# A state-space layer with a ReGLU network behind it: order and size of the first weight transfers, and the engine of one cast

## The chip, the cores and the metric

The kernel runs on one core of a Trainium2 chip. The core has TensorE (PE, the matrix engine, with its weight loads PEld), VectorE (DVE), ScalarE (ACT), GpSimd (POOL) and SyncE (SP), which run their own instruction streams beside each other, and 16 DMA engines that all queues share. The metric is the device time of one execution in microseconds (us).

## The reference, cut to what matters

Two stages. The first is a chunked state-space layer (batch 4, 8 heads, 768 positions, head size 32, state size 16). The second takes its output as 3072 tokens of 256 features through a gated network with 1536 hidden features.

```python
# first stage, per chunk of positions: cum = cumulative sum of log(a)
L = np.exp(cum[:, :, :, None] - cum[:, :, None, :]) * causal
CB = np.einsum('bhin,bhjn->bhij', Cc, Bc)
y_intra = np.einsum('bhij,bhjd->bhid', CB * L, xc)
y_inter = np.einsum('bhin,bhnd->bhid', Cc, state) * np.exp(cum)[:, :, :, None]
y[:, :, sl] = y_intra + y_inter
state = decay_full[:, :, None, None] * state + np.sum(Bx, axis=2)
...
# second stage
gate = np.maximum(x @ w_gate, 0.0)
val = x @ w_val
return (gate * val @ w_out).astype(np.float32)
```

All inputs and the output are float32; the kernel multiplies in bfloat16.

## The kernel before, in words

**Stages.** The 3072 tokens are 12 *pairs* of 256 (a pair is two chunks of 128) and 6 *blocks* of 512 (two pairs). The first stage turns B, C and x of a pair into `yT`, the transposed bfloat16 input of the second stage. For a pair, B and C are scaled by decay factors (`scale_bc`, tile `bs`), transposed on TensorE (`transp`, line 389) and copied out as `BT` and `CT` (`bevac`, `cevac`); `G` (line 452) makes the products `g` of all position pairs; `gevac` copies them out as `gs` with the causal mask, quarter 0 and half of quarter 1 by ACT (lines 464 and 472) followed by POOL's `affine_select` (line 171, "the selects"), the rest by DVE in one instruction per piece (line 475). `Dm` (line 630) multiplies `gs` with x, `inter` (line 610 or 619) adds what the running state gives, `astep` (line 509) and `sevac` carry the state on, and `yevac` copies the sum into `yT`.

**The second stage** runs, for a block, over 12 *steps* f of 128 hidden features: gate and value matmuls, ReLU on ACT, the product on DVE into `h`; then `fout` (line 783) multiplies `h` with `wo`. `gv` (line 738) does a step for 512 tokens, `gvh_mm` (line 753) for 256. In block 0 the first half of steps 0 to 3 is woven into the first stage of pair 1, the second half follows, and then steps 4 to 11 run for 512 tokens each in the order of f.

**Weights.** They lie in DRAM as float32 and are cast to bfloat16 in the transfer, on POOL's DMA queue. `weights(g)` (line 150) loads group g of gate weights, then group g of value weights; a group is 256 columns, that is steps 2g and 2g+1, in a tile of its own `[128, 2, 256]`. `w_tile(ws, f, k)` picks the 128 columns of step f from its group. `weights_out` (line 160) loads a third of `wo`. A matmul that reads a tile waits until the whole transfer into that tile has landed.

**Order.** `in_order` (line 15) ties every instruction to the one before it on its engine, so the program's text is the order on each engine, POOL's DMA issues among them. SP's queue carries a, B, C and x; ACT issues three of pair 0's and pair 1's loads. On POOL the text gives, for the start: the masks; groups 0 and 1 (line 226, held until the first scan of a is done by the small cast in line 225); the cast of x of pair 0, first half (line 845, with `x_cast`, line 841; the second half is DVE's, line 844); two selects of pair 0; a quarter of `scale_bc` of pair 1 (line 893); `weights(2)` and the gate part of group 3 (lines 894 and 895); two selects of pair 1; the value part of group 3, groups 4 and 5 (lines 922 to 924); the three parts of `wo`; then the scaling of pairs 2 and 3, the zeroing of three tiles, and the cast of x of pair 2. On ACT the text has, around line 845: the copies of `BT` and of half of `CT` of pair 0, then the first `gs` cast of pair 0, the copy `bx`, the second `gs` cast. x of pair 1 is issued by SP in `load_x1` (line 866) and cast by ACT in line 921.

Of the kernel before, what the change touches and what calls it, by code (L numbers as in the profile page):

```python
# [9 lines left out]
BF16 = mybir.dt.bfloat16  # L10
# [19 lines left out]
def kernel(  # L30
# [13 lines left out]
    nc = tc.nc  # L44
# [5 lines left out]
    DM, DF = moe_w_gate.shape  # L50
    T = NB * S
    NF = DF // 128
# [5 lines left out]
    glob = ctx.enter_context(tc.tile_pool(name="glob", bufs=1))  # L58
# [78 lines left out]
    def new_xb(p):  # L137
        xb = att.tile([128, 2 * NH * D], BF16, tag="xb", name="xb", bufs=6)
        st.setdefault(p, {})["x"] = [xb[:, i * NH * D:(i + 1) * NH * D] for i in range(2)]
# [3 lines left out]

    wgs, wvs = ([glob.tile([128, 2, 256], BF16, name="%s%d" % (w, g)) for g in range(NF // 2)]
                for w in ("wg", "wv"))
    wo = glob.tile([128, NF, DM], BF16)

    def weights(g, which=(0, 1)):  # L150
        for k in which:
            w, src = ((wgs, moe_w_gate), (wvs, moe_w_val))[k]
            nc.gpsimd.dma_start(
                out=w[g],
                in_=src[:, g * 256:(g + 1) * 256].rearrange("(k p) f -> p k f", k=2))

    def w_tile(ws, f, k):
        return ws[f // 2][:, k, f % 2:256:2]

    def weights_out(f0, f1):  # L160
        nc.gpsimd.dma_start(
            out=wo[:, f0:f1].rearrange("p (g j) m -> p g (j m)", j=2),
            in_=moe_w_out[f0 * 128:f1 * 128, :].rearrange("(g p j) m -> p g (j m)", p=128, j=2))
# [32 lines left out]
    w = mm.tile([128, 512], FP32, tag="y", name="w")  # L196
# [27 lines left out]

    nc.gpsimd.tensor_copy(out=wgs[0][0:1, 0, 0:1], in_=cp_first[0:1, 0:1])
    weights(0)
    weights(1)

    fac = glob.tile([128, NB, NC, 2, 8], FP32)
# [78 lines left out]
    def new_bs(p):  # L308
        st[p]["bs"] = att.tile([128, 4, 128], BF16, tag="bs", name="bs", bufs=6)
        bs = st[p]["bs"]  # L310
        if p < NWIDE:
            st[p]["tin"] = [[bs[:, 2 * j + r] for r in range(2)] for j in range(2)]
        else:
            st[p]["tin"] = [[bs[:, 2 * i + j] for i in range(2)] for j in range(2)]
            st[p]["B"] = st[p]["tin"][0]

    def copy(eng, out, in_):
        (eng.copy if eng is nc.scalar else eng.tensor_copy)(out=out, in_=in_)  # L318
# [15 lines left out]
    def scale_bc(p, eng, js=slice(0, 2), f=None, ts=(0, 1)):  # L334
        b, c0, _ = place(p)
        src, dst = views(p, js)
        if f is None:
            if p < NWIDE:
                f = wfac[:, p, js].rearrange("s j r h -> s (j r) h")
            else:  # L340
                f = fac[:, b, c0:c0 + 2].rearrange("s c j h -> s (c j) h")
        n = f.shape[1]
        for t in ts:
            eng.tensor_tensor(  # L344
                out=dst[:, :, t], in0=src[:, :, t],
                in1=f[:, :, 4 * t:4 * t + 4].to_broadcast([128, n, 4, N]), op=ALU.mult)
# [384 lines left out]
    def gv(b, f, turns=False):  # L731
        if b not in fst:
            fst[b] = ffn.tile([128, NF, 512], BF16, tag="h", name="h")
        tk = slice(b * 512, (b + 1) * 512)
        g, v = bank("gate"), bank("val")
        order = [(g, wgs, 0), (g, wgs, 1), (v, wvs, 0), (v, wvs, 1)]
        for o, ws, k in sorted(order, key=lambda e: e[2]) if turns else order:
            nc.tensor.matmul(out=o, lhsT=w_tile(ws, f, k), rhs=yT[:, k, tk],  # L738
                             start=(k == 0), stop=(k == 1), skip_group_check=True)
        r = ffn.tile([128, 512], BF16, tag="r", name="r", bufs=4)  # L740
        nc.scalar.activation(r, g, AF.Relu)  # L741
        nc.vector.tensor_tensor(out=fst[b][:, f], in0=r, in1=v, op=ALU.mult)  # L742

    def gvh_mm(b, f, u):
        if f == 0 and u == 0:
            fst[b] = ffn.tile([128, NF, 512], BF16, tag="h", name="h")
        tk = slice(b * 512 + u * 256, b * 512 + (u + 1) * 256)
        gv_ = (mm.tile([128, 2, 256], FP32, tag="y", name="gv") if b + f == 0 else
               bank("gv", (128, 2, 256)))
        jk = [(j, k) for j in range(2) for k in range(2)]  # L750
        early = b + f + u == 0
        for j, k in sorted(jk, key=lambda v: v[1]) if early else jk:
            nc.tensor.matmul(out=gv_[:, j], lhsT=w_tile((wgs, wvs)[j], f, k), rhs=yT[:, k, tk],  # L753
                             start=(k == 0 and not (early and j)), stop=(k == 1),
                             skip_group_check=True)
        fst[b, f, u] = gv_
# [84 lines left out]
    def x_cast(p, i, eng):  # L841
        copy(eng, st[p]["x"][i], st[p]["xr"][:, i].rearrange("s h d -> s (h d)"))

    x_cast(0, 1, nc.vector)
    x_cast(0, 0, nc.gpsimd)
    new_bs(1)
    keep_warm(1)
    keep_warm(1, 256)
# [42 lines left out]
    scale_bc(1, nc.vector, C_)  # L891
    scale_bc(1, nc.vector, B_, ts=(0,))
    scale_bc(1, nc.gpsimd, B_, ts=(1,))
    weights(2)
    weights(3, (0,))
    new_xb(1)
    Dm(0, "shared")
    inter(0, 1)
# [20 lines left out]
    gevac(1, early=True, between=lambda: backevac(1, nc.scalar))  # L919
    for i in range(2):  # L920
        x_cast(1, i, nc.scalar)
    weights(3, (1,))
    weights(4)
    weights(5)
    weights_out(0, 4)
    weights_out(4, 8)
    weights_out(8, NF)
# [26 lines left out]
    for w in range(W3):  # L954
        nc.scalar.copy(
            out=fac[:, :, 2 * w:2 * w + 2, 1, :].rearrange("p b i h -> p i b h"),
            in_=dall[:, :, w])
# [198 lines left out]
```

## Time and profile before

| what | value |
|---|---|
| median of 3 runs | 122.5 us (122.35, 122.5, 123.0) |
| the profiled execution, whole | 122.54 us |
| its span in the trace | 120.8 us |
| DMA moved in the span | 13.69 MB in 80591 packets |
| q1, SP's queue | 10.54 MB, 58.5% of 16 engines' span |
| q0, POOL's queue | 2.36 MB, 14.1% |
| gate and value transfers | 12 of 128 KB (bfloat16), median 5.0 and 5.1 us from issue to landing |
| `wo` transfers | 3 of 256 KB, median 7.1 us |

Times in the trace count from the start of the span. A timeline line gives start, duration, engine, line of the kernel, operation, tiles written and read, and in brackets how long the engine was idle before it and what ended that idle time. `POOLq`, `SPq` and `ACTq` are the DMA issues of the engines; an issue's own duration is the time the engine spends on it, not the time of the transfer. "To landing" is the time from the start of the issue until the last part of the transfer has arrived.

### The profile page before, as it was taken

The numbers are of one execution on the slowest core, as the hardware profiler recorded it, in microseconds if no ns is written. First come the engines' busy times: TensorE is split into PE (matmuls) and PEld (weight loads), VectorE is DVE, ScalarE is ACT, GpSimd is POOL, SyncE is SP. The second block draws the span as 40 slices with busy tenths as digits, with TensorE's granted clock in tenths as the row PEclk, the third lists the DMA queues.
The fourth block names the chain that finished last, engine by engine and source line by source line (L and its number), as shares of the span: only waits on it lengthen the run. The fifth ranks groups of instructions, "written<-read, shape, count | busy, mean of one in ns | idle before, by whom it ended". The sixth has DMA issues, their size and how long they took to land.

```text
span 120.8 us, 3330 instructions
## 1 busy us (share of the span) xinstructions
PE 116.8 (97%) x1238; PEld 75.1 (62%) x1238; DVE 89.2 (74%) x214; ACT 74.3 (61%) x161; POOL 51.4 (43%) x104
## 2 busy tenths in 40 slices
PE   7999999999999999999999999999999999999990
PEld 2446854577885477888487544578444677444790
DVE  5898879986999956899875687856778675678500
ACT  4077886752998734888734767526767445766240
POOL 6879999741805342957076273333400033000000
PEclk9999999999999999999999999999999999999999
DMA  2999999999998999999986799962200002200022
GB/s 57 215 186 176 192 173 197 211 144 127 159 125 151 133 101 109 121 242 134 98 148 121 84 122 149 194 130 82 91 5 0 0 0 92 87 0 0 0 87 87
DMA packets 80591, 13.69 MB, mean 113 GB/s; under 512 B 73424, under 2 KB 80576, under 8 KB 80576
## 3 DMA queue, kind: packets, MB, share of 16 engines
q1 hardware_dynamic: 73088, 10.54, 58.5%
q0 software_dynamic: 4080, 2.36, 14.1%
q10 hardware_dynamic: 3408, 0.59, 2.6%
q8 instruction: 9, 0.15, 0.5%
q14 instruction: 6, 0.05, 0.1%
HBM read 11.12 MB, written 3.15 MB: 118 GB/s over the span
## 4 chain that ended last, share of the span: by engine, by line
PE 94%; DVE 3%; ACT 0%; issue 0%; DVEq 0%
PE o L783 26%; PE gate L738 19%; PE val L738 19%; PE gv L753 13%; PE w L200 3%; PE g L452 2%; PE g L491 2%; PE y L678 1%; PE y L630 1%; PE o L795 1%; PE tp L389 1%; DVE gs L475 1%; DVE bs L344 1%; PE y L619 1%; PE y L665 0%; PE dw L236 0%
## 5 line engine op out<-in xcount | busy, mean ns | idle before, releaser
L742 DVE TENSOR_TENSOR h<-r,val 128x512 bf16<-128x512 bf16 x54 | 36.7, 687 | 9.3 <-ACT r L741 6.4
L741 ACT ACTIVATE r<-gate 128x512 bf16<-128x512 f32 x54 | 32.2, 597 | 11.9 <-PE gate L738 10.9
L783 PE MATMUL o<-wo,h 128*128 128x256 bf16 x276 | 33.6, 273 | 0.0
L738 PE MATMUL val<-yT,wv 128*128 128x512 bf16 x108 | 32.6, 379 | 0.0
L738 PE MATMUL gate<-yT,wg 128*128 128x512 bf16 x108 | 32.6, 379 | 0.0
L783 PEld LDWEIGHTS <-h 128*128 128x128 bf16 x276 | 25.8, 98 | 5.5 <-issue 1.2
L171 POOL TENSOR_SCALAR_AFFINE_SELECT gs<-gs 128x512 bf16<-128x512 bf16 (+1 forms) x24 | 12.2, 533 | 24.9 <-ACT gs L464 24.9
L475 DVE TENSOR_TENSOR gs<-g,masks 128x512 bf16<-128x512 f32 x24 | 15.4, 685 | 5.9 <-PE g L491 2.8
L738 PEld LDWEIGHTS <-wv 128*128 128x128 bf16 x108 | 10.6, 98 | 12.5 <-DMA wv<-in_moe_w_val_dram 0.2
L738 PEld LDWEIGHTS <-wg 128*128 128x128 bf16 x108 | 10.4, 98 | 11.1
L464 ACT CAST gs<-g 128x512 bf16<-128x512 f32 x12 | 7.0, 587 | 14.7 <-PE g L452 6.4
L763 DVE TENSOR_TENSOR h<-r,gv 128x256 bf16<-128x256 bf16 x36 | 13.9, 417 | 0.9 <-ACT r L760 0.7
L760 ACT ACTIVATE r<-gv 128x256 bf16<-128x256 f32 x36 | 13.7, 389 | 1.2
L753 PE MATMUL gv<-yT,wg 128*128 128x256 bf16 x72 | 13.9, 273 | 0.0
L753 PE MATMUL gv<-yT,wv 128*128 128x256 bf16 x72 | 13.9, 272 | 0.0
L297 POOL TENSOR_TENSOR bz<-bcr,fac 128x512 bf16<-128x512 f32 x6 | 6.4, 1059 | 10.5 <-DMA bcr<-in_B_dram 10.5
L811 ACT COPY ob<-o 128x512 f32<-128x512 f32 x11 | 6.5, 592 | 4.1 <-PE o L783 4.0
L318 ACT CAST yT<-y 128x512 bf16<-128x512 f32 (+1 forms) x9 | 4.6, 531 | 5.4 <-PE y L678 3.4
L753 PEld LDWEIGHTS <-wv 128*128 128x128 bf16 x72 | 7.0, 98 | 0.8
L753 PEld LDWEIGHTS <-wg 128*128 128x128 bf16 x72 | 6.8, 98 | 1.1 <-issue 0.2
L200 PE MATMUL w<-const-bfloat16-1.0 128*128 128x512 bf16 (+3 forms) x16 | 6.0, 497 | 0.8 <-PEq L1140 0.8
L318 DVE CAST yT<-y 128x256 bf16<-128x256 f32 (+1 forms) x7 | 3.7, 548 | 4.0 <-PE y L678 2.0
(119 smaller groups left out, 112.0 us busy)
## 6 DMA issues: line engine op xcount, KB each, us to landing
xr<-in_x_dram SPq DMA_DIRECT2D x23, 128.0 KB, 3.2
out_dram<-ob SPq DMA_DIRECT2D x9, 256.0 KB, 2.7
bcr<-in_B_dram SPq DMA_DIRECT2D x16, 64.0 KB, 3.0
bcr<-in_C_dram SPq DMA_DIRECT2D x16, 64.0 KB, 2.9
wg<-in_moe_w_gate_dram POOLq DMA_DIRECT2D x6, 128.0 KB, 5.0
wv<-in_moe_w_val_dram POOLq DMA_DIRECT2D x6, 128.0 KB, 5.1
wo<-in_moe_w_out_dram POOLq DMA_DIRECT2D x3, 256.0 KB, 7.1
out_dram<-ob SPq DMA_DIRECT2D x4, 128.0 KB, 2.3
```

Of the source, the lines that this page charges most:

```text
L171: nc.gpsimd.affine_select(out=dst, in_=dst, pattern=pattern, compare_op=ALU.is_ge, fill=0.0, base=0, channel_multiplier=-1)
L200: nc.tensor.matmul(out=w[:, 0:cols], lhsT=nc.const_aps.tensor(1.0, [128, 128], BF16), rhs=nc.const_aps.tensor(1.0, [128, cols], BF16), sta ...
L318: (eng.copy if eng is nc.scalar else eng.tensor_copy)(out=out, in_=in_)
L464: nc.scalar.copy(out=d[:, 0], in_=g[0])
L475: nc.vector.tensor_tensor(out=d[:, q], in0=g[q], in1=m, op=ALU.mult)
L738: nc.tensor.matmul(out=o, lhsT=w_tile(ws, f, k), rhs=yT[:, k, tk], start=(k == 0), stop=(k == 1), skip_group_check=True)
L741: nc.scalar.activation(r, g, AF.Relu)
L742: nc.vector.tensor_tensor(out=fst[b][:, f], in0=r, in1=v, op=ALU.mult)
L753: nc.tensor.matmul(out=gv_[:, j], lhsT=w_tile((wgs, wvs)[j], f, k), rhs=yT[:, k, tk], start=(k == 0 and not (early and j)), stop=(k == 1), ...
L760: nc.scalar.activation(r[:, 0:256], fst[b, f, u][:, 0], AF.Relu)
L763: nc.vector.tensor_tensor(out=fst[b][:, f, u * 256:(u + 1) * 256], in0=fst.pop((b, f, u, "r"))[:, 0:256], in1=fst.pop((b, f, u))[:, 1], op ...
L783: nc.tensor.matmul(out=o[:, ts % 2], lhsT=fst[b][:, f, ts * 128:(ts + 1) * 128], rhs=wo[:, f], start=(f == 0 and new), stop=(f == NF - 1), ...
```

## The change

Three edits, all in the start of the kernel.

- The first half of x of pair 0 is cast by ACT (`nc.scalar`) and no longer by POOL.
- The gate weights of group 2 (steps 4 and 5) are issued on POOL at that place, ahead of the selects of pair 0. The value part of group 2 and all of group 3 are issued ahead of pair 1's selects.
- The groups are no longer all alike: `WG` holds their limits, and the last group has 512 columns, steps 8 to 11, so that gate and value of these steps come in one transfer each. `w_tile` finds the columns of a step in the wider tile.

```diff
+    WG = [0, 256, 512, 768, 1024, DF]
-    wgs, wvs = ([glob.tile([128, 2, 256], BF16, name="%s%d" % (w, g)) for g in range(NF // 2)]
-                for w in ("wg", "wv"))
+    wgs, wvs = ([glob.tile([128, 2, u - l], BF16, name="%s%d" % (w, g))
+                 for g, (l, u) in enumerate(zip(WG, WG[1:]))] for w in ("wg", "wv"))
...
             nc.gpsimd.dma_start(
                 out=w[g],
-                in_=src[:, g * 256:(g + 1) * 256].rearrange("(k p) f -> p k f", k=2))
+                in_=src[:, WG[g]:WG[g + 1]].rearrange("(k p) f -> p k f", k=2))
 
     def w_tile(ws, f, k):
-        return ws[f // 2][:, k, f % 2:256:2]
+        g = min(f // 2, len(ws) - 1)
+        o = f // 2 * 256 - WG[g]
+        return ws[g][:, k, o + f % 2:o + 256:2]
...
     x_cast(0, 1, nc.vector)
-    x_cast(0, 0, nc.gpsimd)
+    x_cast(0, 0, nc.scalar)
+    weights(2, (0,))
     new_bs(1)
...
     scale_bc(1, nc.gpsimd, B_, ts=(1,))
-    weights(2)
-    weights(3, (0,))
+    weights(2, (1,))
+    weights(3)
     new_xb(1)
...
     for i in range(2):
         x_cast(1, i, nc.scalar)
-    weights(3, (1,))
     weights(4)
-    weights(5)
     weights_out(0, 4)
```

## The prediction

> **What bounds the kernel now.** I read first the share of busy time, the strip of forty slices and the chain that ended last, on the page.
>
> ```profile
> span 120.8 us, 3330 instructions
> PE 116.8 (97%) x1238; PEld 75.1 (62%) x1238; DVE 89.2 (74%) x214; ACT 74.3 (61%) x161; POOL 51.4 (43%) x104
> ...
> DMA  2999999999998999999986799962200002200022
> ...
> PE 94%; DVE 3%; ACT 0%; issue 0%; DVEq 0%
> ```
>
> TensorE sets the end: 94% of the chain is its own work, 3% is DVE's. The DMA strip is at 9 from about 3 to 60 us, so transfers compete while the weights come in. The change touches only the first 26 us. There I read the chain in order of time, the pieces between 8 and 21 us:
>
> ```profile
> 7.21 1.19 DVE gs L475 x2
> 8.42 0.42 DVE gs L479
> 8.93 0.83 DVE bs L344 x3
> 9.76 0.35 DVE yT L318
> 10.11 0.51 DVE CT L415 x2
> 10.66 0.40 PE g L452 x8
> ```
>
> From 7.21 to 10.66 us DVE sets the pace, one instruction behind the other; from 10.66 on every piece is TensorE's. So an edit on POOL or ACT before 10.66 pays only if it shortens that DVE row, and one after it only if TensorE stands still for it. Does it stand still for weights? In the timeline of weight loads around step 8:
>
> ```profile
> 18.29 0.31 PEld L738 LDWEIGHTS <-wg 128*128 128x128 bf16 x2
> 18.72 0.31 PEld L738 LDWEIGHTS <-wv 128*128 128x128 bf16 x2
> 19.15 0.31 PEld L738 LDWEIGHTS <-wg 128*128 128x128 bf16 x2
> 19.70 0.20 PEld L738 LDWEIGHTS <-wv 128*128 128x128 bf16 x2 [0.23 <-DMA wv<-in_moe_w_val_dram]
> ```
>
> The loads come every 0.43 us, so the last was due at 19.58 and started at 19.70: value weights of steps 8 and 9 were late. It is the only wait for a weight transfer in the list of waits. But the matmuls in the timeline start at 19.37 (gate), 19.80 (val), 20.23 (gate), 0.43 apart as before: the loads run ahead and the lateness was swallowed. So **no time is lost to weights in this execution**, and there is nothing in that wait to win.
>
> **When the weights land.** The issue's start (timeline) plus its time to landing (DMA view of a window holding that issue) gives, in us: gate 2 (steps 4, 5) 9.56+5.2 = 14.8, value 2 10.32+5.4 = 15.7, gate 3 11.03+6.0 = 17.0, value 3 12.74+4.9 = 17.6, gate 4 13.45+4.9 = 18.4, value 4 14.16+5.5 = 19.7, gate 5 14.87+5.5 = 20.4, value 5 15.58+5.7 = 21.3, then the three parts of wo 16.29+6.3 = 22.6, 17.04+7.1 = 24.1, 17.77+7.6 = 25.4. First loads are at 15.81, 16.13, 17.43, 17.86, 19.15, 19.58 (due), some 21.3 and 21.5. The eight narrow ones land (21.3-14.8)/7 = 0.93 us apart, while POOL issues them 0.74 apart: the queue's service sets the times. The three of wo, twice as many bytes each, land (25.4-21.3)/3 = 1.36 apart.
>
> **The change, part by part.**
>
> *x of pair 0 from POOL to ACT.* POOL and ACT in their timelines:
>
> ```profile
> 6.12 0.75 POOL L153 DMA_DIRECT2D wv<-in_moe_w_val_dram  x1
> 6.83 0.44 POOL L318 CAST xb<-xr 128x256 bf16<-128x256 f32 x1
> 7.76 1.03 POOL L171 TENSOR_SCALAR_AFFINE_SELECT gs<-gs 128x512 bf16<-128x512 bf16 x2 [0.48 <-ACT gs L464]
> 9.10 0.51 POOL L344 TENSOR_TENSOR bs<-bcr,wfac 128x128 bf16<-128x128 f32 x1 [0.30 <-DVE wfac L884]
> 9.56 0.77 POOL L153 DMA_DIRECT2D wg<-in_moe_w_gate_dram  x1
> ```
>
> ```profile
> 6.08 0.48 ACT L413 ACTIVATE CT<-tp,tmask 128x256 bf16<-128x256 bf16 x1
> 7.10 0.59 ACT L464 CAST gs<-g 128x512 bf16<-128x512 f32 x1 [0.54 <-PE g L452]
> ...
> 12.08 0.73 ACT L318 CAST xb<-xr 128x256 bf16<-128x256 f32 x2
> ```
>
> ACT stands 0.54 us before its gs cast at 7.10, waiting for the g matmuls. The added cast costs 0.73/2 = 0.37 by the last row; x itself landed at 2.20+3.9 = 6.1. It runs from about 6.5 to 6.9, under that wait, so its cost is 0 with 0.17 to spare. Without the cover, the gs cast, bx and the second gs cast behind it on ACT start up to 0.37 later, and POOL's selects and Dm of pair 0 after them. The first reader of the cast is the state matmul at 8.13, well after either end. POOL loses 0.44, but its select at 7.76 waits for ACT anyway: no gain.
>
> *Gate 2 ahead of the selects.* One issue, 0.74 us, takes the cast's place: 6.83 to 7.57, before the select at 7.76. Cost 0, with 0.19 to spare; the slowest issue in the trace (0.93, the first one) would end at 7.76. Queued behind it are the two selects, which Dm of pair 0 (8.60 on PE) waits for; those 0.19 us are the cover, and what it exceeds them by goes into Dm. A rule speaks against this place: the Trainium skill, "SBUF — State Buffer", section "SBUF: two separate sides", says that VectorE's fast copies lock GpSimd out of the SBUF port with which it writes descriptors. DVE casts x in fp32 from 6.46 to 6.98, so by the rule the issue would start in earnest at 6.98 and end at 7.72 to 7.91, at most 0.15 us on top of the sum. The trace so far disagrees: the issue at 6.12 ran for 0.41 us beside that very cast and took 0.75 us, not more than the others.
>
> Behind the selects the issues are value 2, gate 3, value 3 at 9.56, 10.3, 11.03 in place of gate 2, value 2, gate 3: the same count ahead of pair 1's selects at 11.76, so these don't move.
>
> The transfer moves as well, past x of pair 1 on SP's queue (issued 7.02 and 7.41, landed at 10.7 and 11.3). That x is cast by ACT from 12.08 and 12.45. Gate 2 takes at most one place of its queue, 0.93 to 1.31 us (the spacing above, and its largest, from gate 4 to value 4). If all of it came first, the second half of x would land at 12.2 to 12.6, which is 0 to 0.17 us late. Two queues share the engines, so a part of it comes after; I take 0 and keep 0.2.
>
> *Steps 8 to 11 in two transfers for four.* Before, six narrow transfers from 9.56 on brought gate 2 to value 4. Now three narrow ones (value 2, gate 3, value 3) land in the places of the first three, 14.8, 15.7 and 17.0, needed at 16.13, 17.43, 17.86: their slack grows to 1.4, 1.7 and 0.8 us. Then come two wide ones, 256 KB each, issued at 12.74 and about 13.5 (0.77 us apiece, as wo's issues). The trace has no wide gate; wo is the nearest row, of the same size and on the same queue. By it: gate 17.0+1.36 = 18.4 (needed 19.15), **value 18.4+1.36 = 19.8 (needed 19.6)**. That is as late as now (19.7), and 0.1 later. Matmuls took in 0.12 us before, so I take +0.05. The bound below: the wide ones keep the narrow spacing, 17.0+2x0.93 = 18.9, no wait and 0 gained. The bound above: cost goes by bytes, 2x0.93 = 1.86 apiece, so value lands at 20.75 and the load is 1.17 us late, about 1.05 past what was swallowed. All of that is TensorE's, because after step 8 it has no other slack. Steps 10 and 11 then have their weights with steps 8 and 9.
>
> *What follows on POOL.* Two issues fewer put wo at 14.3 instead of 16.3 and all behind it (scaling of pairs 2 and 3, the zeroing) some 2 us earlier. The first wo is used at 23.1 and landed at 22.6, so nothing waited there. x of pair 2, late now (14.49+9.5 and 15.69+10.1 = 25.8, with POOL waiting 2.4 us), is cast by 26.5 and first needed at 27.96; weights that end sooner can only bring it forward. Worth 0.
>
> **Sum**: 0 (cast) + 0 (issue) + 0 (x of pair 1) + 0.05 (wide value) + 0 (POOL) on the profiled execution, 122.54 us (span 120.8 and 1.74 around it): 122.6. The median of the three runs is 122.5, 0.04 below that execution, so I don't shift it. By the bounds alone it lies between 122.5 and 122.54+1.05+0.2+0.15 = 123.9.
>
> **The rivals.**
>
> 1. *No change* (forecast), 122.6. For it: each moved piece has a cover in the rows. Against: four covers of 0.1 to 0.2 us are thin.
>
> 2. *The wide value transfer stops TensorE at step 8*: slower, 123.6. Steps 8 and 9 now wait for bytes that only steps 10 and 11 use. It decides from the spacing at which the second wide one lands: the stall is 17.0 + 2s - 19.7, over 0.6 us from s = 1.65. Against it: wo came at 1.36 on average. For it: the step from the first to the second wo was 1.5, and while x of pair 1 is pushed back into the stretch from 11 to 13 us, where the two queues already hold 63% and 61% of the engines, the third place may slip past 17.0 as well. Price +1.05.
>
> 3. *Pair 1 starts late*, as x of pair 1 or the select of pair 0 slips: +0.2 to +0.35 over the forecast, 122.8 to 123.0.
>
> 4. *Faster*, about 121.9. The three runs go from 122.35 to 123.0; if the executions without a profile lose 0.6 us to late weights of steps 4 to 7 (slacks 1.0, 0.4, 0.4 and 0.2 us now), the wider slacks would end that. Against it: the profiled execution is as long as the median and loses nothing there, and the wide value transfer has no more slack than before.
>
> 5. *The change isn't what it says*: gate 2 issued at 6.83 but held by the queue, landing at 14 as before. The first four landed 3.9 to 4.0 us after their issue, so this is unlikely, and would cost nothing: 122.5.
>
> **How the numbers follow.** The bound for a change that this kernel's measurement can tell from none is 0.5%, 0.6 us: below 121.9 is faster, above 123.1 slower. Forecast 0.42; rival 2 0.26; rival 3 0.13, of which 0.04 past the bound, when it adds to a late value transfer; rival 4 0.14; rival 5 0.05. Faster is 0.14; slower 0.26+0.04 = 0.30; the same is 0.56. The likeliest alone spans 122.3 to 122.9 (the spread of the runs). The range reaches down to rival 4's 121.9 and up to rival 2's 123.6.
>
> **What would show it.** Right: in the changed kernel POOL issues gate 2 before 7, its first select still starts at 7.7 to 7.8, ACT's gs cast at 7.1, g of pair 1 at 10.7; the gate of step 8 starts at 19.3 to 19.5 and its value loads wait at most some 0.3 us; no other load waits for weights. Wrong, slower: a wait of over 0.7 us on wv at step 8, or ACT's xb cast of pair 1 waiting for a DMA. Wrong, faster: the step 4 matmuls start before 15.5, by which a link of the DVE row that I call untouched has become shorter.

## The result and the profile after

The changed kernel takes 124.01 us (median of 4 runs, 123.83 to 124.54) against 122.53 us: a ratio of 1.0121, 95% interval 1.0086 to 1.0157. It is slower, by 1.5 us; the forecast was no change, and the time lies above the range. Every ratio here and below compares only executions within 1.5% of the fastest of their kernel. The profiled execution took 124.54 us, 2.0 more than that of before. From the page, and the chain between 12 and 30 us (start, length, what):

```profile
span 122.8 us, 3328 instructions
...
PE 77%; DMA 9%; POOL 3%; DVE 3%; SPq 3%; issue 1%; ACT 0%; POOLq 0%; DVEq 0%
```

```profile
12.13 1.58 SPq L86
...
13.75 11.36 DMA bcr<-in_B_dram
...
25.24 1.20 POOL bs L347 x2
26.44 0.58 POOL bz L292
...
27.26 1.85 POOL bz L292 x2
29.11 0.57 POOL xb L321
...
29.72 0.24 PE A_ps L512 x4
```

TensorE's share of the chain fell from 94% to 77%. What came in is not a weight: it is one load on **SP's** queue, B of pair 3 (the last `bcr` load before x of pair 2). It was issued at 13.75 and landed at 25.1; before, it was issued at 11.25 and landed 7.7 later, at 19.0. POOL waited for it, and behind it in POOL's order came the scaling of pair 3, the three zeroings, and the cast of x of pair 2, which the state matmul needs. In the kernel before, SP's issue and POOL's scaling (pair 3 is its second half) and cast were:

```profile
11.25 3.19 SPq L86 DMA_DIRECT2D bcr<-in_B_dram  x1
```

```profile
18.45 2.41 POOL L344 TENSOR_TENSOR bs<-bcr,wfac 128x256 bf16<-128x256 f32 x4
...
25.89 0.61 POOL L318 CAST xb<-xr 128x512 bf16<-128x512 f32 x1 [2.37 <-DMA xr<-in_x_dram]
```

TensorE's timeline after the change shows the two places where it stood, at the transposes tp of pair 3 and at the state matmul A_ps of pair 2:

```profile
25.34 0.40 PE L455 MATMUL g<-CT,BT 32*128 32x256 bf16 x8
26.50 0.40 PE L392 MATMUL tp<-ident,bs 128*128 128x128 bf16 x4 [0.76 <-POOL bs L347]
...
29.72 0.21 PE L512 MATMUL A_ps<-xb,bx 128*32 128x64 bf16 x4 [0.65 <-POOL xb L321]
```

Before, the same steps were:

```profile
25.12 0.40 PE L452 MATMUL g<-CT,BT 32*128 32x256 bf16 x8
25.45 0.40 PE L389 MATMUL tp<-ident,bs 128*128 128x128 bf16 x4
...
27.96 0.21 PE L509 MATMUL A_ps<-xb,bx 128*32 128x64 bf16 x4
```

From g to tp it went from 0.33 to 1.16 us (+0.83), from tp to A_ps from 2.51 to 3.22 (+0.71), and from A_ps to the block of state matmuls (line 569, now 572) from 1.47 to 1.72 (+0.25). With 0.22 that TensorE was late at g already, that is 2.01, the whole difference of the spans.

The bookkeeping of the landing is as simple: from landing to state matmul the chain above takes 29.72-25.11 = 4.61 us, and before that matmul started at 27.96. So B of pair 3 could land as late as 27.96-4.61 = **23.35 us** at no cost; it had 4.4 us to spare before, and was 1.8 us past it after.

The places that the prediction named, in the changed kernel's timelines of POOL, ACT and the weight loads:

```profile
6.97 0.75 POOL L154 DMA_DIRECT2D wg<-in_moe_w_gate_dram  x1
7.88 1.03 POOL L174 TENSOR_SCALAR_AFFINE_SELECT gs<-gs 128x512 bf16<-128x512 bf16 x2 [0.15 <-ACT gs L467]
```

```profile
6.57 0.40 ACT L321 CAST xb<-xr 128x256 bf16<-128x256 f32 x1
7.21 0.59 ACT L467 CAST gs<-g 128x512 bf16<-128x512 f32 x1 [0.25 <-PE g L455]
...
12.84 0.41 ACT L321 CAST xb<-xr 128x256 bf16<-128x256 f32 x1 [0.18 <-DMA xr<-in_x_dram]
```

```profile
20.06 0.18 PEld L741 LDWEIGHTS <-wv 128*128 128x128 bf16 x2 [0.25 <-DMA wv<-in_moe_w_val_dram]
```

The issue and the cast lie in their gaps as forecast (everything here is 0.11 us late from the first loads on, ahead of the change). x of pair 1 is late for its cast by 0.18 us, which costs TensorE 0.22 us in Dm of pair 1. The wide value transfer is 0.25 late, and as before this was swallowed: the gates of steps 8 and 9 start 0.86 apart.

### The profile page after: what moved, and what is told of

It reads as the page before. It is cut to its first block, busy times and chain, and to the rows that moved or that the text cites. A ratio compares the mean times of both kernels' runs of the same rounds, so it can differ in the third digit from the quotient of the medians.

```text
span 122.8 us, 3328 instructions
## 1 busy us (share of the span) xinstructions
PE 117.3 (95%) x1238; PEld 75.3 (61%) x1238; DVE 89.4 (73%) x214; ACT 74.8 (61%) x162; POOL 49.6 (40%) x101
## 4 chain that ended last, share of the span: by engine, by line
PE 77%; DMA 9%; POOL 3%; DVE 3%; SPq 3%; issue 1%; ACT 0%; POOLq 0%; DVEq 0%
PE o L786 22%; PE gate L741 16%; PE val L741 16%; PE gv L756 10%; DMA bcr<-in_B_dram 9%; PE w L203 3%; SPq L86 3%; POOL bz L292 2%; PE g L494 2%; PE y L681 1%; PE g L455 1%; PE o L798 1%; PE y L633 1%; POOL bs L347 1%; DVE gs L478 1%
## 5 line engine op out<-in xcount | busy, mean ns | idle before, releaser
L174 POOL TENSOR_SCALAR_AFFINE_SELECT gs<-gs 128x512 bf16<-128x512 bf16 (+1 forms) x24 | 12.2, 532 | 25.6 <-ACT gs L467 25.6
```

The costliest lines, as they stand in the source:

```text
L174: nc.gpsimd.affine_select(out=dst, in_=dst, pattern=pattern, compare_op=ALU.is_ge, fill=0.0, base=0, channel_multiplier=-1)
```

## The experiments

They ran on three chips, whose own times for the kernel before were 123.24, 122.68 and 123.58 us, so only ratios are compared. First group: the edits one by one. Theory A puts the loss on the wide transfers, theory B on the early gate transfer.

**The wide group alone.**

```diff
+    WG = [0, 256, 512, 768, 1024, DF]
...
     weights(3, (1,))
     weights(4)
-    weights(5)
```

> The kernel before with the wide group alone; cast on POOL and the order of the narrow groups as before. Theory A (bytes of POOL's queue crowd out SP's: while both queues have work they are served about packet for packet, so packets of twice the size and wo issued 0.7 us sooner leave SP fewer turns): B of pair 3 lands at 22 us or later (before: 19.0), POOL's scaling of pair 3 waits for it, and the time rises by 0.7 to 1.4 us, to 123.2 to 123.9. Theory B (the early gate transfer pushes x of pair 1 and all of SP's queue behind it): B of pair 3 lands at 18.5 to 20 and the time stays within 0.3 us of before, 122.3 to 122.8. Step 4 to 7 weights land as before in both.

Measured: ratio 1.0057 (1.0022 to 1.0092). B of pair 3 landed at 24.0. But the loss of this execution at the start has another place; TensorE's timeline:

```profile
19.34 0.59 PE L741 MATMUL gate<-yT,wg 128*128 128x512 bf16 x2
20.91 0.61 PE L741 MATMUL val<-yT,wv 128*128 128x512 bf16 x2 [0.98 <-DMA wv<-in_moe_w_val_dram]
21.35 0.59 PE L741 MATMUL gate<-yT,wg 128*128 128x512 bf16 x2
```

Two gates are 0.86 us apart everywhere else and 2.01 here: 1.15 us lost to the wide value transfer, rival 2 of the prediction. With TensorE that much later, B of pair 3 was in time (it could land up to 28.96-4.61 = 24.35, as A_ps started at 28.96) and tp to A_ps took 2.51 again. So the wide transfers have two effects that cover each other in part.

**The cast and the early gate alone**, six narrow groups.

```diff
-    x_cast(0, 0, nc.gpsimd)
+    x_cast(0, 0, nc.scalar)
+    weights(2, (0,))
...
-    weights(2)
-    weights(3, (0,))
+    weights(2, (1,))
+    weights(3)
```

> The kernel before with the cast on ACT and the gate weights of steps 4 and 5 ahead of pair 0's selects; six narrow groups. Theory A: x of pair 1 lands 1 us or so later and costs 0.2 us, B of pair 3 lands by 21 and POOL does not wait for it past 21; 122.6 to 122.9. Theory B: SP's issues of C and B of pairs 2 and 3 stretch to 1.4 to 1.6 us each as in the changed kernel, B of pair 3 lands at 24 to 25, and the whole loss is here: 123.7 to 124.2.

Measured: 1.0031 (0.9998 to 1.0064). B of pair 3 landed at 20.3, no weight was waited for, and from g of pair 0 to the state matmuls of line 569 it took 22.62 us against 22.74 before: nothing is lost in the start of this execution, against theory B. (Another execution of the same version, further down, did lose there.) The profiled execution lost about 1.1 us at 66 us, where a later x came late; whether that has to do with the change isn't shown.

**The zeroing ahead of the scaling of pair 3**, in the changed kernel.

```diff
+    zero_padded()
     new_bs(3)
     scale_bc(3, nc.gpsimd)
-    zero_padded()
     to_x(2, nc.gpsimd)
```

> The changed kernel with one move: POOL zeroes its three tiles (2.7 us) ahead of the scaling of pair 3 instead of behind it, in the time in which it waits for B of pair 3. If the wait at the head of POOL's order makes the cast of x of pair 2 late, the cast starts at 26.5 to 27.2 instead of 29.1, the wait of the state matmul for it (0.65 us) goes and TensorE's wait for the scaled pair 3 (0.76 us) stays: 123.2 to 123.5. If the cast is late for x itself and not for POOL's order, the time stays at 123.9 to 124.2.

Measured: 1.0038 (0.9999 to 1.0077), a smaller ratio than the changed kernel's, though on another chip. B of pair 3 landed as late as ever, at 25.6, yet the cast of x of pair 2 now waits for x and not for POOL's order, and the state matmul follows tp after 2.51 us (27.00 to 29.51) as before the change:

```profile
25.75 1.19 POOL L347 TENSOR_TENSOR bs<-bcr,wfac 128x256 bf16<-128x256 f32 x2 [3.50 <-DMA bcr<-in_B_dram]
27.55 0.61 POOL L321 CAST xb<-xr 128x512 bf16<-128x512 f32 x1 [0.60 <-DMA xr<-in_x_dram]
```

So that part of the wait was a matter of POOL's order. TensorE still lost 0.39 us before tp, and 1.27 us around step 8 (0.21 before its gate, 1.06 between its gate and the next), as the wide group alone did.

**The cast alone.**

```diff
-    x_cast(0, 0, nc.gpsimd)
+    x_cast(0, 0, nc.scalar)
```

> The kernel before with nothing but the cast of x of pair 0 moved to ACT. Both theories: no change, 122.3 to 122.7; the cast lies under ACT's wait for g, and the first select starts at 7.7 to 7.8 as before. If ACT's queue matters, the first gs cast starts after 7.3 and the time rises by 0.2 or more.

Measured: 1.0020 (0.9985 to 1.0055), and B of pair 3 landed at 18.7. The whole chain from g of pair 0 to line 569 took 22.63 us (before 22.74): the cast costs nothing there.

Second group, all on one chip: both kernels again, and two attempts to take the pressure off.

**The kernel before, again.**

> The kernel before, unchanged, for a profile on the chip that runs the next three. No theory asks for a difference: ratio 1.00; B of pair 3 lands at 18.5 to 20.5.

Measured: 1.0009 (0.9979 to 1.0038), B of pair 3 at 18.8.

**The changed kernel, again.**

> The changed kernel, unchanged, on the same chip: 0.7 to 1.5 us slower than before. Theory A (wide packets on POOL's queue leave SP's queue fewer turns): B of pair 3 lands at 23 to 26 and POOL's scaling of pair 3 ends after 25. Theory C (the loss is that the wide value transfer lands late for step 8): a load of wv at step 8 waits over 0.7 us, and if B of pair 3 is late it costs nothing on top.

Measured: 1.0095 (1.0070 to 1.0121). B of pair 3 landed at 24.5; TensorE lost 0.35 us at step 8, 0.13 before tp, 0.72 before A_ps and 0.25 behind it. Both theories hold a part; x of pair 1 cost nothing this time. What the two queues moved from 15 to 19 us (packets, MB, share of 16 engines), first the kernel before on this chip, then the changed one:

```profile
q0 software_dynamic: 1043, 0.50, 96.5%
q1 hardware_dynamic: 2000, 0.25, 47.5%
```

```profile
q0 software_dynamic: 695, 0.64, 98.5%
q1 hardware_dynamic: 1267, 0.16, 27.3%
```

POOL's queue (q0) holds the engines for nearly the same time in both (the shares of two queues overlap and add up to over 100%). With packets of 1024 B it gets through fewer of them, and SP's queue (q1) moves fewer packets in nearly the same proportion: 1.9 and 1.8 of SP's for one of POOL's. The Trainium skill, "DMA: Bandwidth & Descriptors", section "Queues, rings and completion order", says that each DMA engine takes turns between its queues and switches after a whole packet, typically 9 to 17 descriptors. These two pairs of counts fit turns that go by number and not by bytes, if what the trace counts as a packet is such a descriptor, which no run shows; why SP's queue gets nearly two for one isn't shown either, and over all runs the ratio varies more (table below).

**wo later**, in the changed kernel.

```diff
     weights(4)
+    zero_padded(range(2))
     weights_out(0, 4)
...
-    zero_padded()
+    zero_padded(range(2, 3))
```

> The changed kernel with two of the three zeroings (1.8 us) ahead of the transfers of wo, so that wo is issued at about 16.1 us, as before the change, and not at 14.3. If wo's earlier start is what crowds SP's queue, B of pair 3 lands by 21 and most of the loss goes: within 0.4 us of before. If the wide transfers do it by themselves, B of pair 3 lands at 23 or later and 0.7 to 1.5 us stay lost.

Measured: 1.0038 (1.0004 to 1.0071), less than the changed kernel on the same chip. Yet in the profiled execution, the longest of its ten, B of pair 3 landed at 25.5 and TensorE lost 0.73 us at step 8 and 0.82 before tp: B is late without wo's early start too. Whether the wide transfers or the early gate made it so, this kernel, which has both, doesn't tell; SP's queue moved 1606 packets from 15 to 19 us, as many as in the kernel before (1604). A_ps lost nothing, since two zeroings were out of the way, as in the run with the zeroing first. How much of the gain is wo's and how much the order's isn't told apart.

**B of pair 3 on ACT's queue**, in the changed kernel.

```diff
-    for j in (1, 0):
-        load_bc(3, j, nc.sync)
+    load_bc(3, 1, nc.sync)
...
     nc.scalar.copy(out=ends, ...)
+    load_bc(3, 0, nc.scalar)
```

> The changed kernel with B of pair 3 loaded on ACT's queue, issued at about 9 us, instead of at the end of SP's queue. If the loss goes through B of pair 3 alone, it lands by 16, POOL never waits for it, the cast of x of pair 2 starts when that x lands (26 to 27), and the time is within 0.4 us of before. If SP's queue as a whole is late, x of pair 2 and later loads still come late, and 0.5 to 1.0 us stay lost.

Measured: 1.0055 (1.0025 to 1.0085). B landed in time, and now C of pair 3, the last on SP's queue, came at 24.3 and POOL waited 5.6 us for that; x of pair 1 came 0.88 us late for its cast (0.8 us lost in Dm of pair 1). So SP's queue as a whole is late, not one load.

Third group: the packets' size by itself.

**The wide tile filled by narrow transfers**, in the changed kernel.

```diff
+    def weights_last():
+        for o in (0, 256):
+            for w, src in ((wgs, moe_w_gate), (wvs, moe_w_val)):
+                nc.gpsimd.dma_start(out=w[4][:, :, o:o + 256], in_=...)
...
-    weights(4)
+    weights_last()
```

> The changed kernel with its wide tiles for steps 8 to 11 filled by two transfers of 256 columns each (gate, value, gate, value), so packets of 512 B as before and wo at about 15.8 us; a tile is read only when both of its transfers have landed. If the size of the packets is what crowds SP's queue: in 15 to 19 us SP's queue moves 1700 packets or more (before 2000, changed 1267), B of pair 3 lands by 21 and POOL's wait for it is under 1.5 us; what is left is the wait at step 8 for bytes of steps 10 and 11, 0.5 to 1.2 us. If the early gate transfer or something else in the change crowds it, B of pair 3 lands at 23 or later here too.

Measured: 1.0038 (0.9997 to 1.0080). SP's queue moved 1497 packets, B of pair 3 landed at 23.0, and step 8 waited for nothing: the account by packet size missed on every number, and B came as late as the other account had it. But the run can't separate the two by itself. POOL's transfers here have the size and the order of those in the early gate alone and differ only in the tile they fill, yet in the three profiles of these two versions B of pair 3 landed at 20.3, 23.0 and 24.9: one version varies from execution to execution by as much as was to be shown. In this one 23.0 is under 23.35, and TensorE lost nothing to B; it lost 0.47 us in Dm of pair 1 to a late x of pair 1.

**The early gate alone, again.**

> Cast on ACT and early gate weights alone, narrow groups, again with more rounds. If these two edits cost nothing: ratio 0.998 to 1.003, B of pair 3 lands by 21, no wait for weights. If the early gate transfer carries a part of the loss: ratio over 1.004.

Measured: 1.0022 (0.9990 to 1.0054). Twice the interval reaches 1; with the cast alone at 1.0020, the ratios can't tell a cost of the early gate by itself from none. The profiled execution, the third longest of twelve (124.44 us, over 1.5% above the shortest), missed the expected landing, though. B of pair 3 landed at 24.9 and not by 21, with no wide transfer in the kernel and no wait for weights; POOL's and TensorE's timelines:

```profile
25.00 1.20 POOL L344 TENSOR_TENSOR bs<-bcr,wfac 128x256 bf16<-128x256 f32 x2 [5.78 <-DMA bcr<-in_B_dram]
```

```profile
29.48 0.21 PE L509 MATMUL A_ps<-xb,bx 128*32 128x64 bf16 x4 [0.64 <-POOL xb L318]
```

TensorE lost 0.36 us in Dm of pair 1, then 0.25 before tp, 0.72 before A_ps and 0.24 behind it, as in the changed kernel. So the early gate transfer can make pair 3 late without the wide ones; how often it does isn't shown.

**The wide group alone, again.**

> The wide group alone, again, on the chip of this call. If all of the loss sits in the wide transfers: ratio 1.006 to 1.012, a wait for wv at step 8 over 0.7 us and B of pair 3 at 23 to 25.

Measured: 1.0103 (1.0052 to 1.0155), as large as the whole change. B of pair 3 at 25.1; TensorE lost 0.65 at step 8, 0.25 before tp, 0.71 before A_ps, 0.25 behind it.

**Packets of half the size**, in the kernel with the early gate alone: 128 columns per transfer, twice the issues.

```diff
+    def weights_halves(g):
...
-    weights(4)
-    weights(5)
+    weights_halves(4)
+    weights_halves(5)
```

> Cast on ACT, early gate, and the weights of steps 8 to 11 in transfers of 128 columns, packets of 256 B, twice as many issues (wo at about 18.7 us). If SP's share goes by packets: SP's queue moves 2000 packets or more in 15 to 19 us and B of pair 3 lands at 19 or before. If it goes by bytes or by time, B of pair 3 lands as with packets of 512 B, 19.5 to 21. TensorE may wait for weights and for wo, which come later; its time says nothing on the question.

Measured once: 124.55 us, with waits that the later wo and scaling bring. The queues from 15 to 19 us:

```profile
q0 software_dynamic: 1510, 0.40, 97.5%
q1 hardware_dynamic: 2439, 0.31, 62.1%
```

SP's queue moved 2439 packets, more than ever, while POOL's moved fewer bytes in the same time. B of pair 3, which had the early gate in its way as well, landed at 20.1, not at 19 or before; the count bears the account by packets out, the landing doesn't.

The runs side by side, by the packets that SP's queue moved. Its loads from x of pair 1 to B of pair 3 are six of 128 KB in pieces of 128 B, 6144 packets:

| run | gate early | packet of steps 8 to 11 | SP 7 to 11 us | SP 15 to 19 us | POOL 15 to 19 us | SP 7 to 19 us | B of pair 3 lands |
|---|---|---|---|---|---|---|---|
| before | no | 512 B | 2539 | 1604 | 1056 | 6824 | 19.0 |
| before, again | no | 512 B | 2324 | 2000 | 1043 | 7169 | 18.8 |
| cast alone | no | 512 B | 2343 | 2063 | 1072 | 7316 | 18.7 |
| early gate | yes | 512 B | 1422 | 1757 | 1166 | 6341 | 20.3 |
| early gate, again | yes | 512 B | 1001 | 1823 | 1094 | 5305 | 24.9 |
| wide tile, narrow | yes | 512 B | 1473 | 1497 | 995 | 5359 | 23.0 |
| half packets | yes | 256 B | 978 | 2439 | 1510 | 6094 | 20.1 |
| wide alone | no | 1024 B | 2138 | 1042 | 813 | 6109 | 24.0 |
| wide alone, again | no | 1024 B | 1927 | 1181 | 697 | 5266 | 25.1 |
| changed, again | yes | 1024 B | 1618 | 1267 | 695 | 5292 | 24.5 |
| changed | yes | 1024 B | 925 | 1258 | 590 | 4957 | 25.1 |
| changed, zeroing first | yes | 1024 B | 1501 | 1089 | 600 | 4928 | 25.6 |
| changed, wo later | yes | 1024 B | 1523 | 1606 | 688 | 5562 | 25.5 |

With the early gate SP moved 925 to 1618 packets from 7 to 11 us, without it 1927 to 2539. From 15 to 19 us it moved 1042 to 1267 beside wide transfers (1606 with wo later) and 1497 to 2063 beside narrow ones. For one packet of POOL's SP moved 1.6 beside packets of 256 B, 1.5 to 1.9 beside 512 B, and 1.3 to 2.3 beside 1024 B. Where SP is through with some 6800 by 19 us, B of pair 3 is there. Where it isn't, what is left competes with the transfers of wo, also in packets of 1024 B (in half packets these are issued only at 18.7 us), and B lands at 20 to 26. The early gate alone and the wide group alone each did this in at least one execution, and the same version varies by several us.

## Why the prediction was wrong, point by point

- **The cast on ACT and the early issue at no cost**: right. The cast ran from 6.57 under ACT's wait for g, the issue from 6.97 to 7.72 ahead of the select at 7.88. The issue ahead of it (6.26 to 7.01) again lay beside DVE's fp32 cast (6.57 to 7.12), this one for 0.15 us, and both took 0.75 us as the others. So no lockout by the rule of the Trainium skill, "SBUF — State Buffer", section "SBUF: two separate sides", is seen here; whether this cast is one of the fast copies that the rule means, no run shows.
- **x of pair 1**: its second half landed at 12.8, for a forecast of 12.2 to 12.6 at the latest. It cost 0.22 us in the profiled execution, nothing in five others with the early gate, and 0.36 and 0.47 in two more (not counting the run with B of pair 3 on ACT's queue). The value 0 was too kind and the bound of 0.2 too small; rival 3, with 0.2 to 0.35, was nearer.
- **The wide value transfer**: landed at 13.57+6.5 = 20.1, for 19.8, and in the profiled execution the stall was swallowed as forecast. That was luck. In five of the six other profiles with wide transfers TensorE lost at step 8: 0.35 us (changed, again), 0.65 and 1.15 (wide alone), 0.73 (wo later) and 1.27 (zeroing first), in two of them more than the bound of 1.05. Rival 2 is real and varies; it isn't what made the profiled execution slow.
- **"What follows on POOL ... Worth 0"**: this is the step that failed. It said that the scaling of pairs 2 and 3 would come 2 us earlier, and that weights which end sooner can only bring x of pair 2 forward. Scaling of pair 3 began at 25.2 instead of about 19.7, and the cast of x of pair 2 at 29.1 instead of 25.9. Its working followed the landings of POOL's own transfers and of x, and left out C and B of pairs 2 and 3 on SP's queue, whose transfers the moved ones pass. It took it that weights that end sooner can only help SP's loads; who gets the engines while both queues have work was not asked. The term is +1.8 us of 2.0 in the profiled execution (0.83+0.71+0.25).
- **The bound above, 123.9**, held the issue, x of pair 1 and the wide value, and nothing for SP's other loads. So the measured 124.01 lies above it, and above the range, which ended at rival 2's 123.6.
- **Faster**: no version had a ratio under 1; TensorE had lost nothing to weights, as the prediction read from the matmuls.

What stays open: how the loss divides in a usual execution between step 8 and pair 3. A late step 8 hides a late pair 3, and the profiles show both divisions. Open too is how much of it the early gate carries: its ratios can't be told from none, while one of its profiles lost as much as the changed kernel. That POOL's transfers hold SP's loads back is shown by the counts; that larger packets do so by taking turns is argued from them, and the range of the ratio is wide. No version that beats the kernel before came out of the experiments; none of them shortens the part of the chain that TensorE already fills.

## What to carry to other kernels

When a transfer is moved or merged, list what shares the DMA engines with it in that stretch on every queue, and for each of those loads its landing, its first reader and the slack through all that the reader's engine has queued behind it. Merging saves issues and engine time, but on engines that are busy throughout it can cost the small packets of another queue their turns, and so can a transfer that is merely moved ahead. Take more than one profile of a version before a landing time is used as evidence: here B of pair 3 landed at 20.3 and at 24.9 in the same one. And lateness that was swallowed (a wait in the weight loads, none between the matmuls) is no gain to be had.

## What the runs showed of the hardware that was not expected

- With both queues at work from 15 to 19 us, SP's queue moved 0.31 MB beside packets of 256 B on POOL's queue, 0.19 to 0.26 MB beside 512 B, and 0.13 to 0.20 MB beside 1024 B. In packets it got 1.6, 1.5 to 1.9, and 1.3 to 2.3 for each one of POOL's (the fences above: 2439 for 1510, 2000 for 1043, 1267 for 695).
- A queue that is behind shows at the issuer: two of SP's issues of `bcr` took 0.58 us each in the kernel before (10.01 and 10.63 us), and the same two 1.43 and 1.58 in the changed one. That a full queue is the reason is argued, not shown.
